# One table, another order: 493 commands of an attention and expert-layer kernel rearranged, helpers on other engines

## The chip, the cores and the metric

One core of a Trainium2 chip. The metric is the device time of one execution in microseconds. The kernel before takes 190.56 us (median of 3 runs, 189.74 to 191.1).

## The reference

Four batches, 8 heads, 768 positions, 64 values per head. Heads 0, 2 and 6 see every earlier position; the other five see 4 sink positions and a window of 64. The result of attention is the input of an expert layer with 3072 tokens, 512 wide in, 768 hidden, 512 out.

```
scores = where(mask, q @ k.T / 8, -1e9)
a = exp(scores - max); a = a / (sum(a) + 1e-9)
x = (a @ v) as [batch * 768, 8 * 64]
h = max(x @ w1, x @ w2, x @ w3)
out = h @ w_out                       # float32
```

## The kernel before

All of the work is a table of short commands, `PROGRAM`, 65 lines of text with 493 commands. A loop at the end of the kernel takes them one by one and calls a helper for each. An engine runs its instructions in the order in which the commands issued them, and waits on semaphores for what it reads; so the table's order is the order on every engine, and a letter at a command's end names the engine that does it (d VectorE, a ScalarE, p GpSimd, r VectorE by a reduction, s SyncE's queue).

The work on one batch goes in two halves of 384 positions (`half` 0, 1). Batch 0 has commands of its own, since nothing can be hidden behind it:

- `hl half hp n` loads queries and keys of a pair of heads in float32 (SP's hardware queue), `cast` makes them 16-bit, `turnp` turns them by PE, and the copy out of PSUM is done by the engines named.
- `load_v b half` loads values on SP's queue. For batch 0 `vc` casts them and `vt` sorts them by products with a 0/1 matrix and copies them to `va`; for later batches `v` does that in one copy, and the load is made of 256-byte packets. `y` prepares `vx`, the values of the five windowed heads beside the sink positions.
- `s0 half u pairs` makes scores and their exponentials (ACT), `k0` a mask on them.
- `kx0` and `kx` copy keys for the sinks and windows.

For all batches: `load b quad [i]` is a casting load (float32 in memory, 16-bit on chip) that GpSimd issues on its software queue; `w i` loads one of the weights on the same queue (0 to 2 are w1, w2, w3 of the reference, in tiles w0t, w1t, w2t, and 3 is w_out); `turn` transposes a loaded quad on VectorE; `s b s` and `k` are scores and masks; `av b half hp` multiplies probabilities with values, divides, and leaves the result transposed, by a transposing DMA where it ends with D, otherwise by `x` on PE. `f b half wi ni` is one hidden unit: four products with weight tile wi (0, 1 or 2; called a w0, w1 or w2 unit below), then a copy (wi 0) or a maximum (wi 1, 2). `g` opens several units at once. `o b half tb` is one output block: six products, a copy from PSUM, a store. `gs` and `gp` make a queue wait until a load has landed. `flags`, `check`, `verdict`, `read` and `guess` test whether the heads and sums are as the program assumes; `read` takes the answer into every engine's registers, and a slow path is taken if it isn't so.

What limits how far a command can run ahead are pools of buffers: four PSUM banks for products, two double banks for scores (`st`), three staging buffers each for keys/queries and for values.

The very last output block of batch 3, half 1 is split by columns, so that the two copies can be made by two engines:

```
for c, n in ((0, 384), (384, DMdl - 384)) if final else ((0, DMdl),):
```

Of the kernel before, what the change touches and what calls it, by code (L numbers as in the profile page):

```python
# [81 lines left out]
LEAST, MOST = 1.0e-9, 16.0  # L82

PROGRAM = (
# [65 lines left out]
)  # L150


# [900 lines left out]
```

## Time and profile before

| | |
|---|---|
| runs | 191.1, 189.74, 190.56 us |
| profiled execution, its own time | 190.84 us |
| its span, first to last instruction | 189.3 us |
| granted clock of TensorE | 0.994 |
| PE busy | 178.8 us (94%) |
| VectorE (DVE) busy | 139.4 us (74%) |
| ScalarE (ACT) busy | 101.2 us (53%) |
| GpSimd (POOL) busy | 82.7 us (44%) |
| hardware queue q1 | 18.19 MB, 40.3% of 16 DMA engines |
| software queue q0 (casting loads) | 7.87 MB, 24.4% |

The profiled execution's time is 1.5 us longer than its span, because the span counts from the first to the last instruction. Its slices show PE at 9 tenths or more almost everywhere but in the first eight of 40 and the last, and the DMA engines nearly full from the second slice to the twentieth:

```profile
PE   6888889899999999999999999999999999999990
DMA  4999999999899999969989321131122032421043
```

In rows of instructions L12 is line 12 of the kernel before; a row of the timeline has start, duration, engine, line, operation, out<-in, how many, and in brackets the idle time before with what ended it.

### The profile page before, as it was taken

The numbers are of one execution on the slowest core, as the hardware profiler recorded it, in microseconds if no ns is written. First come the engines' busy times: TensorE is split into PE (matmuls) and PEld (weight loads), VectorE is DVE, ScalarE is ACT, GpSimd is POOL, SyncE is SP. The second block draws the span as 40 slices with busy tenths as digits, with TensorE's granted clock in tenths as the row PEclk, the third lists the DMA queues.
The fourth block names the chain that finished last, engine by engine and source line by source line (L and its number), as shares of the span: only waits on it lengthen the run. The fifth ranks groups of instructions, "written<-read, shape, count | busy, mean of one in ns | idle before, by whom it ended". The sixth has DMA issues, their size and how long they took to land.

```text
span 189.3 us, 4743 instructions
## 1 busy us (share of the span) xinstructions
PE 178.8 (94%) x1854; PEld 105.0 (55%) x1854; DVE 139.4 (74%) x297; ACT 101.2 (53%) x163; POOL 82.7 (44%) x146
## 2 busy tenths in 40 slices
PE   6888889899999999999999999999999999999990
PEld 2444545666556456755566455856665567455540
DVE  4366999986979999785889976874855768537721
ACT  4579989745695542957438556464555420331020
POOL 7775799704899961125953680205144000000000
PEclk9999999999999999999999999999999999999997
DMA  4999999999899999969989321131122032421043
GB/s 125 313 325 290 214 212 198 170 126 201 150 146 171 161 234 196 259 89 178 283 135 213 78 94 55 24 66 55 21 57 68 0 112 44 115 108 47 0 167 119
DMA packets 44105, 26.60 MB, mean 140 GB/s; under 512 B 31022, under 2 KB 39470, under 8 KB 44078
## 3 DMA queue, kind: packets, MB, share of 16 engines
q1 hardware_dynamic: 39614, 18.19, 40.3%
q0 software_dynamic: 4192, 7.87, 24.4%
q8 instruction: 15, 0.25, 0.5%
q10 hardware_dynamic: 272, 0.20, 0.3%
q14 instruction: 12, 0.10, 0.2%
HBM read 25.17 MB, written 6.29 MB: 166 GB/s over the span
## 4 chain that ended last, share of the span: by engine, by line
PE 79%; DMA 9%; POOL 5%; issue 2%; SPq 2%; DVE 1%; ACT 0%; ACTq 0%; POOLq 0%
PE yy L442 45%; PE yy L472 15%; PE st L682 7%; PE oacc L725 7%; DMA vs<-in_v_dram 6%; POOL pt L378 4%; PE yst L442 3%; DMA qs<-in_q_dram 2%; SPq L206 2%; PE yst L472 1%; POOL vn L505 1%; DVE kx L566 0%; POOL kx L578 0%; POOL qn L220 0%; POOL vx L532 0%
## 5 line engine op out<-in xcount | busy, mean ns | idle before, releaser
L378 POOL TENSOR_TENSOR pt<-pt,kb 128x256 f16<-128x256 f16 (+4 forms) x49 | 42.1, 883 | 43.6 <-ACT pt L699 43.2
L699 ACT ACTIVATE pt<-st 128x1024 f16<-128x1024 f32 (+2 forms) x51 | 43.5, 909 | 31.1 <-PE st L682 31.0
L442 PE MATMUL yy<-xT,w2t 128*128 128x384 f16 x180 | 36.0, 326 | 0.0
L442 PE MATMUL yy<-xT,w0t 128*128 128x384 f16 x184 | 35.0, 326 | 0.0
L442 PE MATMUL yy<-xT,w1t 128*128 128x384 f16 x176 | 34.7, 326 | 0.0
L472 PE MATMUL yy<-woutt,hT 128*128 128x512 f16 (+1 forms) x138 | 31.9, 372 | 0.0
L459 DVE TENSOR_TENSOR acc<-yy,acc 128x384 f16<-128x384 f32 x44 | 24.2, 554 | 9.7 <-PE yy L442 6.7
L459 DVE TENSOR_TENSOR hT<-yy,acc 128x384 f16<-128x384 f32 x45 | 24.8, 556 | 4.7 <-PE yy L442 2.8
L274 DVE STREAM_TRANSPOSE KQ<-kq 128x384 f32<-128x384 f32 x24 | 25.3, 1131 | 0.0
L442 PEld LDWEIGHTS <-w1t 128*128 128x128 f16 x192 | 18.1, 98 | 12.3 <-issue 0.4
L442 PEld LDWEIGHTS <-w0t 128*128 128x128 f16 x192 | 17.8, 98 | 12.8 <-issue 1.1
L442 PEld LDWEIGHTS <-w2t 128*128 128x128 f16 x192 | 17.9, 98 | 11.8 <-issue 0.2
L481 ACT COPY ot<-yy 128x512 f32<-128x512 f32 (+1 forms) x17 | 9.7, 568 | 26.9 <-PE yy L472 24.1
L455 ACT CAST acc<-yy 128x384 f16<-128x384 f32 x31 | 14.6, 491 | 17.1 <-PE yy L442 14.6
L472 PEld LDWEIGHTS <-hT 128*128 128x128 f16 x150 | 14.4, 98 | 14.9
L725 PEld LDWEIGHTS <-pt 128*128 128x128 f16 x472 | 17.0, 97 | 4.3 <-POOL pt L378 1.0
L725 PE MATMUL oacc<-va,pt 128*128 128x65 f16 x392 | 18.8, 193 | 0.0
L732 DVE TENSOR_TENSOR x<-oacc,sums 128x384 f16<-128x384 f32 x32 | 17.8, 557 | 1.1
L378 DVE TENSOR_TENSOR pt<-pt,kb 128x512 f16<-128x512 f16 (+5 forms) x35 | 15.1, 444 | 3.2 <-ACT pt L699 3.1
L637 ACT ACTIVATE pt<-st 128x1024 f16<-128x1024 f32 (+5 forms) x22 | 15.4, 760 | 1.2 <-PE st L616 1.2
L682 PE MATMUL st<-KQ 32*128 32x128 f16 (+2 forms) x342 | 14.9, 257 | 0.0
L725 PE MATMUL oacc<-vx,pt 128*128 128x65 f16 x80 | 11.9, 192 | 0.7 <-POOL pt L378 0.7
(115 smaller groups left out, 184.4 us busy)
## 6 DMA issues: line engine op xcount, KB each, us to landing
out_dram<-ot SPq DMA_DIRECT2D x24, 256.0 KB, 3.0
vs<-in_v_dram SPq DMA_DIRECT2D x18, 256.0 KB, 5.5
ks<-in_k_dram SPq DMA_DIRECT2D x8, 192.0 KB, 5.3
qs<-in_q_dram SPq DMA_DIRECT2D x7, 192.0 KB, 4.5
kq<-in_k_dram POOLq DMA_DIRECT2D x3, 384.0 KB, 6.3
kq<-in_q_dram POOLq DMA_DIRECT2D x3, 384.0 KB, 9.1
kq<-in_k_dram POOLq DMA_DIRECT2D x3, 288.0 KB, 4.8
kq<-in_q_dram POOLq DMA_DIRECT2D x3, 288.0 KB, 6.3
```

The costliest lines, as they stand in the source:

```text
L274: nc.vector.transpose(out=dst.rearrange("c (p j) -> c j p", j=n)[:, j0:j1], in_=src.rearrange("c (j i) -> c j i", i=R),)
L378: engine.tensor_tensor(out=x, in0=x, in1=of_blocks(kb, pattern, rows), op=ALU.mult)
L442: nc.tensor.matmul(begun_units[b, half, wi, ni][:, 0:HALF], w_t[wi][:, ks, ni * P : (ni + 1) * P], xT[b, half, ks].rearrange("p a t -> p ( ...
L455: op(out=acc[b, half, ni], in_=yy[:, 0:HALF])
L459: nc.vector.tensor_tensor(out=acc[b, half, ni] if wi == 1 else hT[b, half, ni], in0=yy[:, 0:HALF], in1=acc[b, half, ni], op=ALU.max,)
L472: nc.tensor.matmul(yo[:, 0:n], hT[b, half, ns][:, tb * P : (tb + 1) * P], woutt[:, ns, c : c + n], start=(ns == 0), stop=(ns == NNB - 1),)
L481: op(out=ot[:, c : c + n], in_=yo[:, 0:n])
L637: nc.scalar.activation(out=pts[0, half, hp, u][:, r0:r1, c0:c1], in_=sts[hp][:, r0:r1, c0:c1], func=AF.Exp, scale=sc,)
L682: nc.tensor.matmul(sts["XY"[g // 2]][:, g % 2, c0 : c0 + n * P], KQ[rows, 0, ki * P : (ki + 1) * P] if kind == "p" else kx[b % 2][quad][ro ...
L699: nc.scalar.activation(out=pts[b, s, xy][:, r0:r1, c0:c1], in_=st[:, r0:r1, c0:c1], func=AF.Exp, scale=sc,)
L725: nc.tensor.matmul(o[:, i, r, 0 : D + 1], at[b, h, kind, ki, qi], vv[:, 0 : D + 1], start=(n == 0), stop=(n == len(todo) - 1), skip_group_ ...
L732: nc.vector.tensor_tensor(out=x, in0=o[:, :, :, 0:D], in1=rc.unsqueeze(3).to_broadcast([P, HB, 2, D]), op=ALU.mult,)
```

## The change

Only the table differs: the same 493 commands stand in another order, and some have another engine's letter. Everything behind it moves up by four lines. The first lines of both tables, cut to those up to the casting loads:

```diff
-    "idle 7, cleark 0 p, hl 0 1 1 ss, hl 0 2 2 ss, cast 0 0 ad, turnp 0 0 da, idle 3, cast 0 1 pp",
-    "turnp 0 1 aa, hl 1 0 2 ss, cast 0 2 pp, s0 0 1 0, clear 0 p, s0 0 1 1, turnp 0 2 dd",
...
-    "turnp 1 0 da, load_v 0 0 0 4 s, vc 0 0 4 d, turnp 0 3 aa, load_v 0 0 4 4 s, vc 0 4 4 a",
-    "hl 1 2 2 ss, idle 1, kx0 0 3 r, s0 0 0 3, s0 1 1 0, cast 1 1 pp, load 1 0",
...
+    "turnp 0 1 da, kx0 0 1 a, s0 0 0 0, hl 0 2 2 ss, cast 0 3 pp, cast 0 2 pp, load_v 0 0 0 4 s, s0 0 0 1",
+    "turnp 0 3 dd, kx0 0 3 d, s0 0 1 0, turnp 0 2 da, s0 0 1 1, vc 0 0 4 p, kx0 0 2 d, load_v 0 0 4 4 s",
+    "hl 1 0 2 ss, vc 0 4 4 p, cast 1 0 dd, s0 0 0 3, s0 0 0 2, vt 0 1 a, vt 0 02 ad, y 0 0 1:4:2 s r",
...
+    "y 0 0 4:5:1 s d, clear 1 d, clear 0 d, y 0 0 1:4:2 r d, s0 0 1 3, av 0 0 1, idle 1, load 1 0, w 0",
...
-    "f 3 1 2 3, o 3 0 2 d, f 3 1 2 0, o 3 0 0 a, o 3 1 0 a, o 3 1 1 a, o 3 1 2 d",
+    "f 3 1 2 1, f 3 1 2 0, f 3 1 2 3, f 3 1 2 4, f 3 1 2 2, o 3 0 0 d, o 3 0 1 a, check, o 3 1 1 a",
+    "verdict, o 3 1 0 a, o 3 1 2 d, o 3 0 2 d, read",
```

GpSimd around batch 1's first casting load (`load 1 0`, the two DMAs into `kq` of 128 rows) and the load of the first weight (tile w0t). `kn` and `qn` are cast pairs, `vs` staged values, `vn` cast values, `pt` probabilities, `vx` and `kx` the copies for sinks and windows. Before:

```order
L220 CAST kn<-ks 128x384
L220 CAST qn<-qs 128x384
L260 DMA kq<-in_k_dram 128x1536
L260 DMA kq<-in_q_dram 128x1536
L220 CAST qn<-qs 128x384
L399 DMA w0t<-in_moe_w_dram 128x4x768
L287 CAST gates<-qs 1x2
L378 TENSOR_TENSOR pt<-pt,kb 128x2x128
```

and now:

```order
L501 CAST vn<-vs 128x768 x2
L216 CAST kn<-ks 128x384
L216 CAST qn<-qs 128x384
L256 DMA kq<-in_k_dram 128x1536
L256 DMA kq<-in_q_dram 128x1536
L395 DMA w0t<-in_moe_w_dram 128x4x768
L216 CAST kn<-ks 128x384
L216 CAST qn<-qs 128x384
L530 COPY vx_149<-va_147 64x8x64
L501 CAST vn<-vs 128x768
L374 TENSOR_TENSOR pt<-pt,kb 128x2x128
L562 COPY kx_152<-KQ 128x2x64
```

The two casts of half 0's values have come to GpSimd, ahead of the casting loads, and the load of w0t follows those at once. The single cast of 128x768 is the first part of half 1's values; before, it stood behind the second quad's loads, on the same engine:

```order
L260 DMA kq<-in_q_dram 96x1536
L399 DMA w1t<-in_moe_w_dram 128x4x768
L505 CAST vn<-vs 128x768
L378 TENSOR_TENSOR pt<-pt,kb 128x1024
L378 TENSOR_TENSOR pt<-pt,kb 128x128
```

Now the cast, a mask and a copy of keys stand ahead of the second quad's loads. On SP's queue the values of half 0 go ahead of the first two pairs of half 1, and the values of half 1 stay the last of batch 0's loads.

The last rows of VectorE, where `ot` is an output block and `yy`, `yst` its PSUM. Before:

```order
L459 TENSOR_TENSOR hT_3263<-yst,acc 128x384
L481 COPY ot<-yy 128x512
L459 TENSOR_TENSOR hT_3280<-yy,acc 128x384
L481 COPY ot<-yy 128x512
L481 COPY ot<-yst 128x384
```

and now:

```order
L784 TENSOR_SCALAR bad<-worst 128x2
L477 COPY ot<-yst 128x512
L792 TENSOR_SCALAR differ<-n,both 1x2
L477 COPY ot<-yst 128x384
L477 COPY ot<-yy 128x512
L797 TENSOR_LOAD differ
```

The split block is no longer the last one: a whole block of 128x512 follows it, and the check of the sums with its read stands among the last copies.

115 rows, old and new, of the table PROGRAM are left out of this document.

## The prediction

> **What bounds the kernel now.** I read the windows first, then the chain of waits, then the DMA queues and the timeline of the places that the chain names. The windows (start:end in us, then busy us of PE, PEld, DVE, ACT, POOL, with granted clock, DMA share and GB/s) say where PE is full:
>
> ```profile
> 5.00:16.00 11.00, 9.33 (x86) 4.76 (x84) 4.90 (x14) 7.91 (x14) 6.97 (x18) 1.00 1.07 325
> 16.00:28.00 12.00, 9.97 (x129) 5.76 (x127) 11.36 (x26) 10.94 (x20) 10.43 (x16) 1.00 1.12 227
> 28.00:36.00 8.00, 7.05 (x98) 4.40 (x96) 7.97 (x12) 7.12 (x16) 7.90 (x11) 1.00 1.13 198
> 36.00:100.00 64.00, 63.99 (x722) 38.64 (x723) 54.59 (x115) 37.23 (x55) 36.47 (x65) 1.00 1.01 178
> 100.00:185.00 85.00, 84.93 (x817) 50.26 (x815) 57.98 (x126) 35.70 (x58) 17.02 (x27) 1.00 0.25 72
> 185.00:189.30 4.30, 0.00 (x0) 0.00 (x0) 0.24 (x1) 0.27 (x1) 0.00 (x0) 0.75 0.37 130
> ```
>
> From 36 to 185 PE is busy 148.92 of 149 us. The table keeps the same 493 commands, so PE's work is the same, and an order can win only ahead of 36 us or in the tail; elsewhere it can only open a stall. What paces the start, the chain says (start, length, what):
>
> ```profile
> 11.51 12.11 DMA vs<-in_v_dram
> 23.74 1.15 POOL vn L505
> 24.89 2.52 POOL pt L378 x3
> 27.41 2.00 issue
> 32.73 3.23 POOL pt L378 x3
> ```
>
> The values of batch 0, half 1, are issued at 11.51 and land at 23.62; POOL casts them and then makes masks. The DMA queues in two windows, 12 to 17 and 17 to 24 (packets, MB, share of 16 engines), say why so late:
>
> ```profile
> q1 hardware_dynamic: 2202, 1.63, 109.2%
> q0 software_dynamic: 7, 0.02, 2.2%
> ...
> q0 software_dynamic: 637, 1.31, 98.4%
> q1 hardware_dynamic: 280, 0.20, 11.5%
> ```
>
> ```profile
> 12.22 0.76 POOL L260 DMA_DIRECT2D kq<-in_k_dram  x1
> ```
>
> Alone, q1 (the hardware queue) moves 1.63 MB in 5 us, 0.326 MB/us. The casting load of batch 1, issued at 12.22, gets almost nothing until 17; after that q1 gets 11.5% and its last 0.20 MB last until 23.6. At its own rate they would have landed near 17.7. So this load costs the values about 6 us.
>
> **The change, part by part.**
>
> *Values of half 0, earlier.* SP now issues them ahead of two pair loads of half 1. Before, they went this way (the last row is the group of POOL's one such cast):
>
> ```profile
> 12.68 0.65 DVE L505 CAST vn<-vs 128x768 f16<-128x768 f32 x1 [0.43 <-DMA vs<-in_v_dram]
> 13.88 0.83 ACT L505 CAST vn<-vs 128x768 f16<-128x768 f32 x1 [0.60 <-DMA vs<-in_v_dram]
> 15.61 1.29 DVE L518 CAST va<-vb 128x512 f16<-128x512 f32 x2 [2.01 <-PE vb L513]
> 17.86 0.67 DVE L518 CAST va<-vb 128x512 f16<-128x512 f32 x1
> 18.89 0.45 PE L725 MATMUL oacc<-va,pt 128*128 128x65 f16 x9
> L505 POOL CAST vn<-vs 128x768 f16<-128x768 f32 x1 | 1.1, 1145 | 1.1 <-DMA vs<-in_v_dram 1.1
> ```
>
> Now POOL casts both pieces, 1.145 us each, about 0.6 us earlier in all, and the sorted values are done near 15 instead of 18.5. The first `av` I put at 17.25 instead of 18.89. That alone pays nothing: what counts is when the w0 and w1 units run.
>
> *Batch 1's first casting load.* On POOL it now stands behind both value casts and behind the pair casts of half 1, whose loads land near 13.9: issue about 14.35, 2.1 us later. The trace has no second case of a casting load behind a full hardware queue, so its first packet is bounded from both sides. If the 4.7 us from 12.22 to 16.92 were a fixed delay, it starts at 19.05; if it was waiting for q1 to drain to a given backlog, it starts at 16.92 as before. With 19.05 the values land near 18, with 16.92 at 23.6 again. At its issue 0.24 + 2.57 × 0.326 = 1.08 MB are ahead of it on q1 now, 1.77 MB before, and q1 is empty near 17.7. If q0 waits for that and then takes the 0.76 us of its issue row, it starts at 18.4, between the ends. I take that: after 12.22 next to nothing came through while q1 held 0.24 MB or more.
>
> *The w0 units.* The page's rows for ACT in this stage:
>
> ```profile
> L637 ACT ACTIVATE pt<-st 128x1024 f16<-128x1024 f32 x10 | 10.1, 1038 | 1.2 <-PE st L616 1.2
> L637 ACT ACTIVATE pt<-st 128x512 f16<-128x512 f32 x5 | 2.9, 611 | 0.0
> L241 ACT COPY KQ<-tr 128x384 f16<-128x384 f16 x7 | 3.2, 492 | 2.0 <-PE tr L238 2.0
> 14.62 1.93 ACT L637 ACTIVATE pt<-st 128x1024 f16<-128x1024 f32 x2
> ```
>
> Exponentials of 1024 follow each other by 0.97, those of 512 by about 0.5, copies by 0.4. Ahead of the first w0 unit ACT has eight, three and five of these, 11.3 us, and another 7.3 us of smaller forms (by the same view): full from 8.4 to 27.0. The turn's matmuls and w0 put the first unit at 27.8, against 27.50 before; but two more score commands are already done, 0.6 us of PE work.
>
> *The w1 units.*
>
> ```profile
> 27.50 0.81 PE L442 MATMUL yy<-xT,w0t 128*128 128x384 f16 x4
> 36.01 0.20 PE L725 MATMUL oacc<-vx,pt 128*128 128x65 f16 x1 [0.65 <-POOL pt L378]
> 36.01 0.54 PE oacc L725 x12
> 36.38 2.11 PE L442 MATMUL yy<-xT,w1t 128*128 128x384 f16 x12
> 34.12 0.72 SPq L285 DMA_DIRECT2D gates<-w1t  x1
> q0 software_dynamic: 1400, 2.40, 111.5%
> ```
>
> Up to the first w1 unit PE has the same commands in both orders but one: `av 0 1 2` (12 products, 0.03 us apart) stood before it, now `av 0 1 3` (21 products) does, 0.28 us more. From 27.8 I count 7.1 us of work without a gap: the 0.65 us for a POOL mask goes, since that mask is now made behind other work. So the first w1 unit stands at 34.95 instead of 36.38, with 0.28 us more done: 1.7 us won. w1 itself landed at 34.1. The casting queue runs at 0.20 MB/us without a pause (last row, 24 to 36 us), and w1 moves with that queue's start: 1.5 us later, less the 11.5% of 7 us (0.8) that q1's packets no longer take, 34.8. With a start at 19.05 it is 35.4 and the gain 1.15 to 1.3. I take **−1.5**. What covers this: ACT has no slack left in that stage; a us more there costs a us.
>
> *36 to 185 us.* Loads of later batches, masks and copies change engine. Adding the rows' durations, DVE gains about 3 us, POOL 7, ACT loses 4; with 139.4, 82.7 and 101.2 busy of 189 none becomes the bound. Between each `turn`, `av` or mask and the PE command that reads it lie about as many PE us as before; the tightest, a value cast of batch 1 on ACT, could cost 0.4, at worst 1. Taken as **0**; cover is the two to four units of 0.65 us that lie between.
>
> *Tail.*
>
> ```profile
> 183.66 0.69 DVE L481 COPY ot<-yy 128x512 f32<-128x512 f32 x1 [3.33 <-PE yy L472]
> 184.43 0.50 PE L472 MATMUL yy<-woutt,hT 128*128 128x128 f16 x6
> 185.01 0.27 ACT L481 COPY ot<-yy 128x128 f32<-128x128 f32 x1 [2.06 <-PE yy L472]
> out_dram<-ot SPq DMA_DIRECT2D x24, 256.0 KB, 3.0
> ```
>
> The last output was split, and its last piece took ACT 0.27 us. Now a whole 128x512 block comes last, copied by DVE in 0.69: +0.42. The check of the sums and the read of its answer move to the very end. A read and its branch take about 1 us on SP and then run under the last store's 3.0 us, so nothing more is added. **+0.45**.
>
> Sum on the profiled execution: 190.84 − 1.5 + 0 + 0.45 = 189.8. It is 0.28 above the median of the runs, 190.56, so I forecast **189.5**.
>
> **The rivals.**
>
> *B, the collision stays (slower).* The casting load begins at 16.92 again and the values land at 23.6. Then POOL casts until 24.8, makes a mask (0.70) until 25.5, copies the far keys until 25.8, and the scores that read them, due at 21.75, come 4 us late. Before, PE idled 0.95 us from 28 to 36 (the window's 7.05 of 8), so between nothing and 0.95 is regained; I count half: the first w1 unit stands at 38.5, 1.85 us behind before's with the 0.28 counted. 190.6 + 1.85 + 0.45 = **192.9**. It decides once the values land past about 19.5; each us beyond costs some 0.8. For it: q1 has the same bytes ahead of the values, and 0.24 MB were left at 16.92. Against: the 2.1 us.
>
> *E, sharing from the first packet.* In the Trainium skill, "DMA: Bandwidth & Descriptors", section "Queues, rings and completion order", each DMA engine goes round-robin, packet by packet, between the queues with work. The trace disagrees for 12 to 17 us: 7 packets against 2202. As a mechanism here: packets begin at 15.1, 0.76 us after the issue, with 0.83 MB of q1 left. In the rows of 17 to 24 a q1 packet has 0.73 KB and a q0 packet 2.06 KB; packet for packet 0.83 MB take 2.5 us alone and the 1140 q0 packets beside them 11.7 at 0.20 MB/us. The values land near 29, so 189.5 + 0.8 × 9.5, **197**.
>
> *F, more is won.* If the whole 1.64 us of the first `av` carries through, w1's landing is the wall: at 34.1 as before, 36.38 − 34.1 + 0.28 = 2.55 us won, 190.56 − 2.55 + 0.45 = **188.5**. For it: ACT's early queue is a sum of means, and a start before 8.4 shifts it whole. Against it: w1 can be at 34.1 only if q0 starts at 16.92 plus 0.8.
>
> *C, a new stall eats the gain.* ACT, full from 8.4 to 34, waits once for a score bank, or a later value cast is late: +1.5, **191.0**; up to 3 if both happen.
>
> **How the numbers follow.** The forecast 0.43, F 0.16, C 0.10, B 0.27, E 0.04. One per cent, 1.9 us, is about what a measurement tells from no change: below 188.65 lie most of F and the lower edge of the forecast, 0.17; above 192.5 nearly all of B, E and the upper part of C, 0.33; the rest, 0.50, is within. The range reaches down to F less 0.7 us for the runs' own spread (189.74 to 191.1), 187.8, and up past B to 194.0 (values at 25 instead of 23.6), without E. The likeliest case alone spans 188.7 to 190.5.
>
> **What would show it.** Right: the values of half 1 land before 19.5; the first w0 unit near 27.8, the first w1 unit near 35.0 with no gap ahead; PE full from 35 to the end; a 0.69 us DVE copy as the last work and one store behind it. Wrong: q0 packets beside q1 before 18 and the values past 20; a POOL cast of values in the chain after 20; w1 after 35; PE gaps past 40 us; a read or branch that ends after the last store.

## The result and the profile after

The changed kernel takes 192.51 us (median of 15 runs, 191.63 to 194.37), the kernel before in the same series 190.22. The ratio is 1.0101, with a 95% interval of 1.0074 to 1.0127: about 1.9 us slower by this ratio of the fast runs; the medians lie 2.3 us apart. I had forecast 189.5, a win of about 1 us. The profiled execution took 192.67 us with a span of 191.2; the one before took 190.84, 1.83 us less.

The windows of the changed kernel, with the columns and limits of the prediction's:

```profile
5.00:16.00 11.00, 9.30 (x82) 4.53 (x82) 5.72 (x14) 7.39 (x14) 6.91 (x14) 0.84 1.06 319
16.00:28.00 12.00, 9.50 (x137) 5.73 (x136) 11.07 (x30) 11.22 (x25) 9.26 (x17) 1.00 1.09 213
28.00:36.00 8.00, 7.33 (x116) 4.88 (x112) 7.88 (x10) 7.14 (x16) 6.05 (x9) 1.00 1.13 208
36.00:100.00 64.00, 62.86 (x713) 37.21 (x702) 54.85 (x108) 38.41 (x57) 40.00 (x62) 1.00 0.97 183
100.00:185.00 85.00, 85.00 (x814) 50.39 (x812) 63.06 (x135) 30.18 (x49) 24.66 (x33) 1.00 0.23 66
185.00:191.20 6.20, 1.17 (x6) 0.32 (x4) 0.88 (x2) 0.22 (x1) 0.00 (x0) 0.80 0.38 135
```

The clock of 0.84 from 5 to 16 us, where the kernel before has 1.00, is not what costs: six of the 15 runs had a granted clock of 1.000, and took 192.05 to 192.82 us.

Three places differ from the forecast. From 36 to 100 us PE was full before; now it lacks 1.14 us. PE works on into the last window. And the start, which was to win 1.5 us, won 0.3 at most: the first w1 unit stands 0.04 us earlier, with the 0.28 us of products more done that the prediction counted. Its steps, from the timeline:

```profile
15.40 0.77 POOL L256 DMA_DIRECT2D kq<-in_k_dram  x1
19.39 0.82 POOL L501 CAST vn<-vs 128x768 f16<-128x768 f32 x1 [0.40 <-DMA vs<-in_v_dram]
28.39 1.47 PE L438 MATMUL yy<-xT,w0t 128*128 128x384 f16 x8
29.93 1.62 DVE L528 COPY vx<-va 64x256 f16<-64x256 f16 x1
31.59 3.99 DVE L270 STREAM_TRANSPOSE KQ<-kq 128x384 f32<-128x384 f32 x4
35.64 0.40 PE L678 MATMUL st<-KQ 32*128 32x256 f16 x5 [0.67 <-DVE sums L726]
35.61 0.73 SPq L281 DMA_DIRECT2D gates<-w1t  x1
36.34 1.95 PE L438 MATMUL yy<-xT,w1t 128*128 128x384 f16 x11
```

The values are clear, as forecast: their cast begins at 19.39 instead of 23.74. But the first scores of batch 1 wait at 35.64. The profile names the reciprocal behind the transposes; the last of these four transposes ends at 35.58. w1 lands only at 35.6: the gate on SP, which waits for it, starts at 35.61. The first w1 unit stands at 36.34, against 36.38 before.

Two things are late, then, and neither by a late start of the casting queue. Its first packet came at 17.09 (before: 16.92), and by 25 us it had moved 1.5 MB in both. But GpSimd issued the second quad's loads and w1 later, behind the value cast, the mask and the copy of keys that now stand ahead of them, and w1 behind one mask more. Before:

```profile
19.75 1.08 POOL L260 DMA_DIRECT2D kq<-in_k_dram  x2
21.82 0.83 POOL L399 DMA_DIRECT2D w1t<-in_moe_w_dram  x1
```

And now:

```profile
21.99 1.08 POOL L256 DMA_DIRECT2D kq<-in_k_dram  x2
25.55 0.83 POOL L395 DMA_DIRECT2D w1t<-in_moe_w_dram  x1
```

From 24 to 28 us the queue moved 0.71 MB instead of 0.85, about 0.7 us at its 0.20 MB/us. What makes up the rest of the 1.5 us by which w1 landed later is not shown; w2's load, issued at 28.49 instead of 30.65 on the same queue, is a candidate. And on VectorE a mask (0.73 us) and the copy of 1.62 us now stand ahead of the second quad's four transposes; before, the last seven of the eight ran without a break from 27.22 to 34.06.

One execution tells only so much here: in six traces whose commands up to the first w1 unit are those of the changed kernel, that unit stands between 35.70 and 37.24 (e5, e13), and in two with those of before at 36.38 and 35.25 (e14). So 0.3 us at the start cannot be told from nothing.

### The profile page after: what moved, and what is told of

It reads as the page before. It is cut to its first block, busy times and chain, and to the rows that moved or that the text cites. A ratio compares the mean times of both kernels' runs of the same rounds, so it can differ in the third digit from the quotient of the medians.

```text
span 191.2 us, 4739 instructions
## 1 busy us (share of the span) xinstructions
PE 178.7 (93%) x1854; PEld 104.2 (55%) x1854; DVE 146.0 (76%) x304; ACT 96.1 (50%) x158; POOL 90.8 (47%) x144
## 3 DMA queue, kind: packets, MB, share of 16 engines
q0 software_dynamic: 4192, 7.87, 23.6%
## 4 chain that ended last, share of the span: by engine, by line
PE 68%; DVE 16%; DMA 4%; issue 4%; POOL 3%; SPq 2%; ACT 1%; POOLq 0%; DVEq 0%
PE yy L438 34%; PE yy L468 13%; PE oacc L721 7%; PE st L678 6%; DVE KQ L270 5%; PE yst L438 3%; DMA qs<-in_q_dram 2%; POOL pt L374 2%; DMA vs<-in_v_dram 2%; DVE hT L455 2%; DVE x L728 1%; PE st L597 1%; PE st L612 1%; SPq L735 1%; DVE pt L374 1%
## 5 line engine op out<-in xcount | busy, mean ns | idle before, releaser
L374 POOL TENSOR_TENSOR pt<-pt,kb 128x512 f16<-128x512 f16 (+5 forms) x56 | 52.5, 955 | 38.8 <-ACT pt L695 36.5
L438 PE MATMUL yy<-xT,w0t 128*128 128x384 f16 x188 | 35.7, 326 | 0.2 <-DVE hT L455 0.2
L438 PE MATMUL yy<-xT,w2t 128*128 128x384 f16 x180 | 35.2, 326 | 0.2 <-DVE acc L455 0.2
L438 PE MATMUL yy<-xT,w1t 128*128 128x384 f16 x172 | 33.2, 326 | 0.1
L451 ACT CAST acc<-yy 128x384 f16<-128x384 f32 x35 | 16.3, 508 | 32.3 <-PE yy L438 30.5
L468 PEld LDWEIGHTS <-hT 128*128 128x128 f16 x150 | 13.7, 98 | 13.9 <-issue 0.2
L633 ACT ACTIVATE pt<-st 128x1024 f16<-128x1024 f32 (+5 forms) x22 | 16.1, 793 | 1.9 <-PE st L612 1.7
L477 DVE COPY ot<-yy 128x512 f32<-128x512 f32 x13 | 8.9, 688 | 6.1 <-PE yy L468 6.1
L477 ACT COPY ot<-yy 128x512 f32<-128x512 f32 (+1 forms) x10 | 5.5, 554 | 15.7 <-PE yy L468 14.1
L678 PEld LDWEIGHTS <-KQ 32*128 32x128 f16 x342 | 8.8, 92 | 8.0 <-issue 6.2
```

Source lines behind the costliest of these rows:

```text
L374: engine.tensor_tensor(out=x, in0=x, in1=of_blocks(kb, pattern, rows), op=ALU.mult)
L438: nc.tensor.matmul(begun_units[b, half, wi, ni][:, 0:HALF], w_t[wi][:, ks, ni * P : (ni + 1) * P], xT[b, half, ks].rearrange("p a t -> p ( ...
L451: op(out=acc[b, half, ni], in_=yy[:, 0:HALF])
L468: nc.tensor.matmul(yo[:, 0:n], hT[b, half, ns][:, tb * P : (tb + 1) * P], woutt[:, ns, c : c + n], start=(ns == 0), stop=(ns == NNB - 1),)
L477: op(out=ot[:, c : c + n], in_=yo[:, 0:n])
L633: nc.scalar.activation(out=pts[0, half, hp, u][:, r0:r1, c0:c1], in_=sts[hp][:, r0:r1, c0:c1], func=AF.Exp, scale=sc,)
```

## The experiments

### The start

The kernel before, with batch 1's first casting load moved behind the last pair casts:

```diff
-    ... cast 1 1 pp, load 1 0, cast 1 3 ap, turnp 1 1 a, w 0 ...
+    ... cast 1 1 pp, cast 1 3 ap, load 1 0, turnp 1 1 a, w 0 ...
```

> The kernel before with one command moved: batch 1's first casting load is issued near 16.9 instead of 12.2, behind the last pair casts. My prediction's reading (the values of half 1 are what paces the start): the values land near 18.5 instead of 23.6, the first w1 unit moves from 36.4 to 35.4 or less, -0.7 to -1.2 us. Rival W (the start is paced by the casting queue itself, whose first packet comes near 17 whatever its issue, then by the transposes and w1's landing): the values land early too, but the first w1 unit stays at 36.2 to 36.8 and the time within 0.3 us of before.

Ratio to before 1.0036 (1.0006 to 1.0066): slower by 0.7 us, if anything. Its timeline:

```profile
17.04 0.76 POOL L260 DMA_DIRECT2D kq<-in_k_dram  x1
23.54 0.94 DVE L505 CAST vn<-vs 128x768 f16<-128x768 f32 x1
32.74 3.04 DVE L274 STREAM_TRANSPOSE KQ<-kq 128x384 f32<-128x384 f32 x3 [1.27 <-DMA kq<-in_q_dram]
36.05 0.72 SPq L285 DMA_DIRECT2D gates<-w1t  x1
36.78 1.46 PE L442 MATMUL yy<-xT,w1t 128*128 128x384 f16 x8
```

The raw trace has the values landing at 18.6 instead of 23.6, yet the w1 units begin at 36.78. The transposes wait for the casting load of the second quad, and w1 comes 1.9 us later than before. So the values, which lead the chain of before with 12.11 us, did not pace the start alone: the transposes, done at 34.06 before, and w1, landed at 34.1, stood next to them, 2.3 us ahead of the first w1 unit. Clearing the values by holding the casting queue back moves the wait only. What clearing them with the queue unmoved would win, this run does not tell, since its first packet came 1.6 us later here.

The changed kernel, with the same load moved forward, ahead of the casts of half 0's values:

```diff
-    "hl 0 1 1 ss, ... cast 0 2 pp, load_v 0 0 0 4 s, ... av 0 0 1, idle 1, load 1 0, w 0, ..."
+    "hl 0 1 1 ss, ... cast 0 2 pp, load 1 0, load_v 0 0 0 4 s, ... av 0 0 1, idle 1, w 0, ..."
```

> The changed kernel with batch 1's first casting load issued near 11 to 12 instead of 15.4, ahead of the casts of half 0's values. Rival B of the prediction: the values of half 1 land at 22.5 to 24 instead of 19.3, the first w1 unit moves back by 2 us or more, +2 us against the changed kernel. Theory W: the queue's first packet stays at 17.0 to 17.1, the values land later, and the first w1 unit moves by no more than 1.2 us.

Ratio to before 1.0482 (1.0438 to 1.0526), 7 us over the changed kernel. The two queues from 14 to 24 us, and what POOL and PE make of it:

```profile
q0 software_dynamic: 754, 1.47, 77.4%
q1 hardware_dynamic: 1222, 0.91, 32.4%
```

```profile
10.72 0.77 POOL L256 DMA_DIRECT2D kq<-in_k_dram  x1
26.28 1.21 POOL L501 CAST vn<-vs 128x768 f16<-128x768 f32 x1 [5.37 <-DMA vs<-in_v_dram]
43.67 1.64 PE L438 MATMUL yy<-xT,w1t 128*128 128x384 f16 x9
```

Rival B of the prediction was the right mechanism at a greater price: values at 26.2, the first w1 unit 7.3 us later. Theory W, with at most 1.2 us, was wrong. The change does steer clear of a real collision; it is just not one that the kernel before pays for in full.

When the casting load's first packet comes can be read over the kernels (raw trace; issue of the load, issue of half 1's values on SP, first packet of q0, bytes of q1 still to come ten packets later):

| kernel | load issued | values issued | first packet | q1 left |
|---|---|---|---|---|
| e11 | 10.72 | 12.42 | 13.50 | 1.28 MB |
| e12 | 12.70 | 13.32 | 14.86 | 0.84 MB |
| before | 12.22 | 11.51 | 16.92 | 0.20 MB |
| changed | 15.40 | 12.95 | 17.09 | 0.07 MB |
| e10 | 15.63 | 11.48 | 17.15 | 0.05 MB |
| e8 | 17.04 | 11.77 | 18.49 | 0 |

Issued behind the last hardware load, the casting load comes through when q1 is all but empty, at 16.9 to 17.2, whether it was issued at 12.2 or 15.6; eleven further traces of these runs agree (issues from 12.4 to 15.4, first packets at 16.8 to 17.1). The wait shows in the early issues, 4.0 to 4.7 us; the 1.5 to 2.2 us of the late ones are little more than the 1.45 that e8's load took with q1 almost empty. Issued ahead of the last hardware load, it comes through 2.2 to 2.8 us after its issue, in the middle of q1. The Trainium skill ("DMA: Bandwidth & Descriptors", "Queues, rings and completion order") has each DMA engine take the queues in turn, packet by packet. That does not fit the wait, 7 packets against 2202, unless the casting queue had nothing ready to move by then, which no run tells; with both queues at work the packets are 754 against 1222.

The copy of 1.62 us at 29.93 was tried as a reduction on the same engine:

```diff
-    ... w 2, y 0 1 1:4:2 r d, f 0 0 0 0 a ...
+    ... w 2, y 0 1 1:4:2 r r, f 0 0 0 0 a ...
```

> The changed kernel with one letter: the copy of the windowed heads' values for batch 0, half 1 (the VectorE copy that took 1.62 us from 29.93 on) is made as a reduction on VectorE. Theory L: the copy was long because it stood beside GpSimd's copy and DMA issue; as a reduction it takes 0.3 to 0.5 us, the transposes behind it begin near 30.9 when the casting load of the second quad lands, the first w1 unit stands at 35.6 to 35.7 (w1's landing) instead of 36.34: -0.6 us. Rival: the transposes wait for that load (30.86 was its landing) and not for the copy: they begin at 30.9 all the same but PE waits for w1 or DVE later, and the time falls by less than 0.3.

```profile
30.84 0.42 DVE L806 TENSOR_REDUCE vx<-va 64x256 f16<-64x256 f16 x1
31.29 4.00 DVE L270 STREAM_TRANSPOSE KQ<-kq 128x384 f32<-128x384 f32 x4
```

It takes 0.42 us, and the ratio to before is 1.0095 (1.0060 to 1.0130), as that of the changed kernel. The rival was right by the time. By the trace it is right for this execution only, where the load landed at 31.25 and the transposes began at 31.29; in that of the changed kernel the load had landed at 30.86, and the copy held the transposes until 31.55.

Last, the kernel before with w1 ahead of the second quad on the casting queue, and three w1 units ahead of batch 1's first scores:

```diff
-    ... y 0 0 4:5:1 r a, load 1 1, w 1, gs 1 ...   and   ... s 1 1, k 1 1 X 0 d, ...
+    ... y 0 0 4:5:1 r a, w 1, load 1 1, gs 1 ...   and   ... f 0 0 1 4, f 0 0 1 5, f 0 0 1 3, s 1 1, k 1 1 X 0 d, ...
```

> The kernel before with w1's casting load ahead of the second quad's, and three w1 units ahead of batch 1's first scores. Theory W (the casting queue's order paces the start): w1 lands near 30 instead of 34.1, PE has work while the transposes wait, -0.3 to -1.0 us against before. Rival: the scores of batch 1 come 2 us later and open a gap of their own between 40 and 50, 0 to +1.5.

Ratio 1.0227 (1.0180 to 1.0274). w1 landed at 31.7, but behind the three units PE waited 2.15 us at 37.3 and again for the scores. The rival was right in kind; its price, at most 1.5 us, was too low for the 4.3 measured.

### The middle

In the changed kernel's middle two rows of VectorE and GpSimd stand out, with pauses of PE behind them (0.17 at 53.6 and 0.24 at 55.9 behind the first, 0.66 at 75.25 behind the second):

```profile
45.76 2.77 POOL L374 TENSOR_TENSOR pt<-pt,kb 128x512 f16<-128x512 f16 x2
47.33 1.75 DVE L374 TENSOR_TENSOR pt<-pt,kb 128x1024 f16<-128x1024 f16 x1
48.46 0.98 POOL L482 CAST va<-vs 128x384 f16<-128x384 f32 x1
53.58 0.81 PE L438 MATMUL yy<-xT,w0t 128*128 128x384 f16 x4 [0.17 <-DVE hT L455]
55.93 0.81 PE L438 MATMUL yy<-xT,w2t 128*128 128x384 f16 x4 [0.24 <-DVE acc L455]
69.58 1.03 POOL L530 CAST vx<-vs 64x1024 f16<-64x1024 f32 x1 [12.77 <-DMA vs<-in_v_dram]
75.25 0.20 PE L721 MATMUL oacc<-va,pt 128*128 128x65 f16 x1 [0.66 <-POOL pt L374]
```

The mask on VectorE took 1.75 us here, and 3.30 or 3.31 in four experiments that leave this place alone (e3, e4, e6, e13); there the pause of PE behind it was 1.02. Its kind takes 0.73 elsewhere. GpSimd was working through masks of its own from 45.8 to 48.5. Here the mask ends 0.55 us behind them, at 49.08, and GpSimd's next cast takes 0.98 us. In e3 that cast takes 0.50, another GpSimd mask follows until 49.97, and VectorE's mask ends 0.56 us behind that one:

```profile
47.22 3.31 DVE L374 TENSOR_TENSOR pt<-pt,kb 128x1024 f16<-128x1024 f16 x1
```

To see what matters, I first gave the mask back to GpSimd:

```diff
-    ... load_v 1 0 s, k 1 2 Y 0 d, load 2 0 1 ...
+    ... load_v 1 0 s, k 1 2 Y 0 p, load 2 0 1 ...
```

> The changed kernel with one letter: the mask of 128x1024 that VectorE did from 47.3 on (1.75 us in one profile, 3.31 in two others, 0.73 for its kind elsewhere) goes back to GpSimd, where the kernel before has it. Theory P (VectorE's 16-bit copies and masks are held while GpSimd works through a row of its own instructions): no VectorE instruction over 1.2 us between 44 and 51, PE's gap at 50 to 56 (0.4 to 1.0 us) goes, -0.4 to -1.0 us against the changed kernel. Rival Q (VectorE simply has too much to do there): GpSimd gets 2.1 us more, VectorE 0.73 us less, the gap shrinks by no more than 0.3.

```profile
48.68 4.07 DVE L530 CAST vx<-vs 64x1024 f16<-64x1024 f32 x1
```

Ratio 1.0131 (1.0062 to 1.0199), no better. VectorE had no long mask left at 47, but its next copy took 4.07 us, against 0.70 in the changed kernel, beside GpSimd's masks from 47.1 on; PE paused 1.26 us at 52 and 0.41 at 54. So theory P's sign, no VectorE instruction over 1.2 us, did not come: what was long moved to the next instruction. Then GpSimd's two masks were left out instead, with VectorE's work unchanged:

```diff
-    ... k 1 2 X 0 p, ... y 1 0 1:8:2 s d, k 1 1 Y 0 p, s 1 4 ...
+    ... y 1 0 1:8:2 s d, s 1 4 ...
```

> The changed kernel without two of batch 1's masks on GpSimd (the 128x512 and 128x768 that ran from 45.7 to 48.5), so that these probabilities stay unmasked. Theory P: VectorE's mask of 128x1024 near 47 takes 0.7 to 0.9 us instead of 1.75 to 3.31, and TensorE's gaps at 49 to 56 shrink from 0.4 to 1.0 us to under 0.2. Rival Q: the mask takes as long or the gaps stay, since VectorE is full without it.

```profile
46.85 0.73 DVE L374 TENSOR_TENSOR pt<-pt,kb 128x1024 f16<-128x1024 f16 x1
```

0.73 us, no pause of PE at 49 to 56, and the ratio falls to 1.0044 (1.0005 to 1.0083). Theory P holds for the mask: it was held while GpSimd's masks followed each other. The time is less telling, since GpSimd also has 2.8 us less to do, and PE's pause at 75 shrinks to 0.41. The Trainium skill ("SBUF — State Buffer", "Who interferes with whom") says that a VectorE instruction with two SBUF inputs contends with a GpSimd instruction that reads SBUF, and calls the shared ports an exclusive lock. The trace agrees, and adds that VectorE can be blocked through several GpSimd instructions in a row. Its statement that a reduction does not contend fits the 0.42 us above, though that one run does not prove it.

A mask of the kernel before was to be put beside a GpSimd mask on purpose:

```diff
-    ... s 1 2, k 1 2 Y 0 p, f 0 0 2 2 ... f 0 1 0 2 d, k 1 2 X 0 p, f 0 0 2 5 ...
+    ... s 1 2, k 1 2 Y 0 p, k 1 2 X 0 d, f 0 0 2 2 ... f 0 1 0 2 d, f 0 0 2 5 ...
```

> The kernel before with one mask of 128x512 on VectorE instead of GpSimd, placed so that it runs beside GpSimd's mask of 128x1024 (45.05 to 47.2). Theory P: VectorE's mask is held until GpSimd's ends, 1.2 to 1.8 us instead of 0.43; time 0 to +0.5 us against before. Rival Q: it takes 0.43 to 0.7.

```profile
44.99 0.43 DVE L378 TENSOR_TENSOR pt<-pt,kb 128x512 f16<-128x512 f16 x1 [0.59 <-ACT pt L699]
45.95 2.12 POOL L378 TENSOR_TENSOR pt<-pt,kb 128x1024 f16<-128x1024 f16 x1 [8.32 <-ACT pt L699]
```

The two missed each other by half a microsecond, so this tells nothing on the hold. The ratio was 1.0105 (1.0014 to 1.0197); its cause is not settled.

The pause at 75 us was to go by moving GpSimd's copies of batch 2's values, for which it waited 12.77 us, behind batch 1's masks:

```diff
-    ... k 1 7 Y 1 p, y 2 0 1:8:2 s p, o 0 0 0 a ... v 1 1 2 a, y 2 0 4:5:1 r p, f 1 0 0 3 a ... v 2 0 0 p
+    ... k 1 7 Y 1 p, o 0 0 0 a ... v 1 1 2 a, f 1 0 0 3 a ... y 2 0 1:8:2 s p, y 2 0 4:5:1 r p, v 2 0 0 p
```

> The changed kernel with two commands moved back on GpSimd: the copies of batch 2's values for the windowed heads, for which GpSimd waited 12.8 us until 69.5, stand behind the masks of batch 1 now. Theory L: the masks are done by 72 instead of 75.2, PE's gap of 0.66 us at 74.6 goes, -0.7 us against the changed kernel, and nothing new waits. Rival: the copies come late for batch 2 instead, a gap of the same size shows after 85.

Ratio 1.0194 (1.0134 to 1.0254). The pause at 75 is gone, and one of 1.15 us stands at 87.2. The chain there:

```profile
84.75 1.22 PE yy L468 x6
85.97 2.34 DMA xT<-x
88.31 0.04 issue
88.35 1.78 PE yy L438 x10
```

A transposing DMA is late now: the stall moved, to the place that the rival named, though it is not the copies that PE waits for. On SP's queue three loads of values stand ahead of that DMA; they lasted from 69.82 to 78.03 instead of 69.28 to 72.32. That they wait for staging buffers which the moved copies still hold is likely, but not shown.

### The end

The split block last again, by itself:

```diff
-    "verdict, o 3 1 0 a, o 3 1 2 d, o 3 0 2 d, read",
+    "verdict, o 3 1 0 a, o 3 0 2 d, o 3 1 2 d, read",
```

> The changed kernel with one edit: the split output block is the last one again, the whole block stands ahead of it. Theory L: the copy at the end is 0.27 us instead of 0.69, so -0.4 us against the changed kernel, +1.5 against before. Rival: what the end costs more is the read and its branch behind the last store, then nothing is won (0.0 to -0.1).

With `check`, `verdict` and `read` moved ahead among the last hidden units as well:

```diff
-    ... f 3 1 1 3, f 3 0 2 2, f 3 1 0 0 d, f 3 1 1 0 ... o 3 0 1 a, check, o 3 1 1 a, verdict, o 3 1 0 a, o 3 1 2 d, o 3 0 2 d, read
+    ... f 3 1 1 3, check, f 3 0 2 2, f 3 1 0 0 d, verdict, f 3 1 1 0 ... f 3 1 1 2, read, ... o 3 0 1 a, o 3 1 1 a, o 3 1 0 a, o 3 0 2 d, o 3 1 2 d
```

> The changed kernel with the end of before: check, verdict and read among the last hidden units, the split block last. Theory: 0.42 us by the shorter last copy and 0.2 by the read that no longer stands behind the last store, so TensorE's end to the end of the span shrinks from 5.0 to 4.4 us; -0.6 us against the changed kernel, +1.2 to +1.4 against before. Rival (the end costs nothing but the copy): 4.6 us.

And the changed kernel's end put on the kernel before:

```diff
-    ... f 3 0 2 2, check, ... o 3 0 1 a, verdict, ... read, ... o 3 0 2 d, f 3 1 2 0, o 3 0 0 a, o 3 1 0 a, o 3 1 1 a, o 3 1 2 d
+    ... f 3 0 2 2, ... o 3 0 1 a, ... f 3 1 2 0, o 3 0 0 a, check, o 3 1 1 a, verdict, o 3 1 0 a, o 3 1 2 d, o 3 0 2 d, read
```

> The reverse: the kernel before with the end of the changed one. Theory: TensorE's end to the end of the span grows from 4.4 to 5.0 us, +0.6 us against before. Rival: 4.8 us, +0.4.

The last product of PE in the four kernels with the spans 191.2 (changed), 191.4 (e3), 192.2 (e13) and 189.1 (e14), in this order:

```profile
184.38 1.79 PE L468 MATMUL yy<-woutt,hT 128*128 128x128 f16 x12
```

```profile
186.41 0.50 PE L468 MATMUL yy<-woutt,hT 128*128 128x128 f16 x6
```

```profile
187.27 0.50 PE L468 MATMUL yy<-woutt,hT 128*128 128x128 f16 x6
```

```profile
182.28 1.79 PE L472 MATMUL yy<-woutt,hT 128*128 128x128 f16 x12
```

From PE's end to the end of the span that is 5.0 us in the changed kernel, 4.5 with the split block last, 4.4 with the old end, and 5.0 with the new end on the kernel before, whose own is 4.4. So 0.5 us belong to the block's order and 0.1 to the read. In the times, whose intervals are about 1 us either way, it does not show: 1.0103 (1.0051 to 1.0155) for e3, 1.0129 (1.0074 to 1.0184) for e13, 1.0012 (0.9977 to 1.0046) for e14. e13 also lost 0.74 us where PE waits for the check.

### The whole

Start and rest were exchanged. The commands ahead of the first w1 unit in the new order, the others in that of before:

> The commands up to the first w1 unit stand in the new order with the new helpers, everything behind in the order of before (its tail too). Theory L (three local losses: the start wins 0.3 us only, the middle loses 1.1, the end 0.65): first w1 unit near 36.3, PE full behind it, time 0.0 to -0.5 us against before. Rival G (the new order is slower in general, by the clock or by more work): a third or more of the loss shows here too, +0.5 us or more.

And the reverse:

> The reverse: the start in the order of before, everything behind the first w1 unit in the new order. Theory L: PE idles about 1.1 us between 40 and 80 us and the end takes 0.65 us longer, +1.7 to +2.3 us against before. Rival G: about half of the loss, +0.5 to +1.2.

The ratios are 1.0130 (1.0078 to 1.0183) and 1.0144 (1.0084 to 1.0203). Together that would be 2.7%, the change has 1.0: each half was fitted to the other. Theory L's number fits e2 within its interval and misses e1 by far; G's fits e1 and misses e2. In e1 PE is full from 40 us on, so its loss lies in the start: PE waits 1.29 us for the transposes at 36.4, and the first w1 unit stands at 38.06.

The same for order and helpers. First the new order with before's letters:

> The new order with the helpers' letters of before: 150 of 493 commands go back to their engine. Theory O (the order costs, by the casting queue at the start, by GpSimd's wait for batch 2's values and by the end): +1.5 us or more against before. Theory H (the helpers cost: GpSimd with 8 us more of masks and VectorE held beside it): within 0.7 us of before.

Then before's order with the new letters:

> The order of before with the new letters. Theory O: within 0.7 us of before. Theory H: +1.2 us or more, with VectorE masks of over 1 us beside GpSimd and gaps on PE between 40 and 80.

1.0928 (1.0871 to 1.0985) and 1.0491 (1.0430 to 1.0552). Neither theory has both runs so slow. In e9 PE waits 4.0 us once for ScalarE, which stands in front of values that have not landed; in e10 2.2 us for a transposing DMA. A command's engine and its place are one choice here.

Last, the changed kernel with its local causes mended and no work left out:

```diff
-    ... w 2, y 0 1 1:4:2 r d ... load_v 1 0 s, k 1 2 Y 0 d, load 2 0 1, k 1 2 X 0 p ... k 1 1 Y 0 p, s 1 4, v 1 0 2 a, v 1 0 0 p ... o 3 1 2 d, o 3 0 2 d, read
+    ... w 2, y 0 1 1:4:2 r r ... load_v 1 0 s, k 1 2 X 0 d, k 1 2 Y 0 d, load 2 0 1 ... s 1 4, v 1 0 2 a, v 1 0 0 p, k 1 1 Y 0 p ... o 3 0 2 d, o 3 1 2 d, read
```

> The changed kernel with four commands edited and no work left out: one mask of batch 1 goes from GpSimd to VectorE, the next one on GpSimd moves behind a values cast, the copy at 30 us is made as a reduction, and the split block is the last again. Theory (three local causes): VectorE's mask of 128x1024 takes 0.7 us, no PE gap at 49 to 56 over 0.2 us, TensorE's end to the end of the span 4.5 us, time -1.0 to -1.6 us against the changed kernel, within 0.8 us of before. Rival (the order itself costs): the time stays at +1.5 us or more against before, with gaps elsewhere.

```profile
36.00:100.00 64.00, 63.75 (x725) 38.08 (x717) 54.78 (x111) 39.46 (x59) 40.09 (x64) 1.00 1.00 186
100.00:185.00 85.00, 85.00 (x811) 50.20 (x809) 62.52 (x133) 29.11 (x47) 23.63 (x30) 1.00 0.24 66
47.48 1.37 DVE L374 TENSOR_TENSOR pt<-pt,kb 128x512 f16<-128x512 f16 x2
```

190.88 us against 190.94, ratio 0.9998 (0.9958 to 1.0039). The two masks together take 1.37 us, PE lacks 0.25 us instead of 1.14, and the loss is gone. Four edits were made at once, but two of them had won nothing alone (e3, e4), so the two masks are what is left; PE's pauses at 53.6 and 55.9 are gone. The distance at the end was 4.8 us in this execution, less of a gain than expected, and the first w1 unit stands at 36.42, as before. No version here beats the kernel before.

## Why the prediction was wrong, step by step

- **What paces the start.** Wrong, and this is the step that failed: the term of −1.5 us, which was 0.3 at most. I read the 12.11 us of the chain as the price of the late values, but the chain names only the last wait. With the values clear, PE waited 0.67 us for the second quad's transposes, done at 35.58 instead of 34.06, and w1 landed at 35.6 instead of 34.1. The sum tied w1 to the casting queue's start and left the transposes out. The queue started as before; what moved were the issues on GpSimd, 2.2 us later for the second quad and 3.7 for w1, and on VectorE the mask and the copy ahead of these transposes. That is read from the traces; no experiment gave these loads their old place in the changed kernel.
- **Batch 1's first load.** Issued at 15.40, not 14.35, because the pair loads behind half 0's values landed later. Its first packet came at 17.09, not 18.4: the case that I had called draining to a given backlog, and for which I had put the values at 23.6. They were clear all the same (19.3), so that was luck. At 17.0 us q1 had 0.22 MB left, and 0.21 before; why this rest landed 4.3 us sooner now is not shown.
- **The w0 and w1 units.** 28.39 instead of 27.8, and 36.34 instead of 34.95: no 7.1 us of work without a gap, but a wait for the transposes. The bound that I gave for w1, 35.4 with a late start, is near the 35.6 by chance only, since the queue did not start late. Won 0.3 us instead of 1.5.
- **36 to 185 us.** Taken as 0, at worst 1; it was 1.6, and the reason that I gave for cover was wrong. I counted busy time and distance in units. A VectorE mask beside GpSimd's took up to 3.31 us instead of 0.73. The trace of before had shown this once (a 128x128 mask of 1.11 us at 34.92), and I passed it over. The profile's 1.14 us of idle time are too few: it counts a pause from the modelled end of a product, while the next product usually starts 0.16 us before that end. From start to start, beyond the usual distance, the three pauses are 0.34 us at 53.6, 0.40 at 55.9 and 0.82 at 75.25.
- **The end.** +0.45 forecast, 0.6 measured from PE's end; right in mechanism, 0.1 to 0.2 short for the read.
- These make −0.3 + 1.6 + 0.6 = 1.9 us; the two spans differ by 1.83.
- **The rivals.** B's time, 192.9, is near what was measured, but its mechanism did not act: the values were clear. That the time came near it is luck. C, a new stall, did act, together with the lost gain. B itself was shown real by e11, at 7 us rather than 3.

## What to carry to other kernels

The longest row of a chain is the wait that came last, not its price: before costing its removal, list what else the same work waits for and when the change issues it, since the next wait bounds what can be won. When masks or copies move between VectorE and GpSimd, look at which of them run at the same time, not at the sums of busy time. And in a program whose engines run in order, a helper and its place in the table go together: either alone cost 5 to 9% here.

## What the runs showed of the hardware that I had not expected

A casting load that is issued behind a row of hardware loads can get next to nothing until that row is nearly drained (issued at 12.2, first packet at 16.9), while one issued ahead of the last of them took 77% of the DMA engines' time beside it in e11, and that load landed at 26.2 instead of 19.3.

A VectorE mask or copy beside GpSimd masks that followed each other took 1.75 us in the changed kernel, 3.31 in e3 and 4.07 in e5, instead of 0.70 to 0.73.

The granted TensorE clock was 0.980 to 0.989 in all six runs of e1, and 0.991 to 1.000 in the seventeen runs of the kernel before beside it. The profile of e1 has 0.86 from 16 to 28 us, where the kernel before has 1.00. The order at the start alone does not explain it: the changed kernel has the same commands there, and 0.984 to 1.000 in its fifteen runs. What causes it was not tried.
